# One row of the second MLP matrix in two pieces: 80 partitions on five DMA engines early, 48 as the last transfer

## The chip, the cores and the metric

The kernel runs on one core of a Trainium2 chip. The metric is the device time of one execution in microseconds, the median over runs. TensorE (PE) multiplies matrices and has a separate path that loads weights (PEld); VectorE (DVE), ScalarE (ACT) and GpSimd (POOL) do the rest of the arithmetic; SyncE (SP) issues all the DMAs of this kernel. A DMA is carried out by up to 16 DMA engines, each of which takes a share of it and works through its own queue in order.

## What is computed

The reference is a gated sum of an attention branch over a sliding window of cached keys and values (one query per sequence, 8 sequences, 32 query heads on 16 key heads, the last 2048 positions) and a small MLP:

```python
def _A_ref(x, k_cache, v_cache, wq, wo):
    W = min(4096, max(256, Sk // 4))            # 2048 of 8192
    q = (x @ wq).reshape(B, Sq, Hq, Dh).transpose(0, 2, 1, 3)
    k = jnp.repeat(k_cache[:, :, Sk - W:, :], rep, axis=1)
    v = jnp.repeat(v_cache[:, :, Sk - W:, :], rep, axis=1)
    p = _softmax(jnp.einsum("bhqd,bhkd->bhqk", q, k) * (Dh ** -0.5), axis=-1)
    o = jnp.einsum("bhqk,bhkd->bhqd", p, v)
    return o.transpose(0, 2, 1, 3).reshape(B, Sq, Hq * Dh) @ wo

def _B_ref(x, w1, b1, w2, b2):
    y = _layernorm(x, axis=-1)
    h = _gelu(jnp.einsum("bsd,df->bsf", y, w1) + b1)
    return jnp.einsum("bsf,fd->bsd", h, w2) + b2

g = _sigmoid((x * gate_w).sum(-1, keepdims=True))
return g * _A_ref(...) + (1 - g) * _B_ref(...)
```

Here D is 576 and F, the width of the hidden layer, is 4608. Everything is bfloat16 in memory.

## The kernel before, in words

The kernel streams some 154 MB through a few buffers of 4 MB each and computes on each as it lands. Queries and the hidden layer of the MLP come first (`q_fn`, `h_fn`). Then 16 items follow, each a 4 MB piece of the key cache and, later, a 4 MB piece of the value cache (`k_item`, `v_item`). At the end come the matrices that only the last step needs: `wo`, the output matrix of the attention, in two halves (`wo_chunk`, L832), and `w2`, the second matrix of the MLP (`m2_chunk`, L858).

`w2` has 4608 rows of 576 numbers. It is laid on 128 partitions with 36 such rows each; "row j" below means the j-th of these 36 on every partition, 128 pieces of 1,152 bytes. `M_CUTS` (L593) cuts the 36 into a piece of 24 rows, and then pieces of 8, 3 and 1. The list `stream` (L594) gives the order of the DMAs:

```python
M_CUTS = [[24], [8, 3, 1]]
stream += [("M", 0), ("W", 0), ("W", 1), ("M", 1)]
```

So after the last value item SP issues the 24 rows, the two halves of `wo` and then 8, 3 and 1 rows. Each issue is chained to the one before (`last_dma`), and waits on SP where its buffer is still being read. `take_slot` gives four buffers in turn; `wo`'s first half has a fifth place of its own.

Every product of the last step adds into one PSUM bank (`BK_ACC`), by `AccGroup` (L570): for each row a pair of matmuls, one for each half of 288 columns, with 8 columns of weights. `o_m2` chains these groups on PE in the order of their transfers, and each waits for its own DMA. When all have ended, DVE (L900) and ACT (L901) copy the two halves to `out_sb`, and SP stores them (L903).

The class `_Plan` (L39) orders the operations of each engine by a simple cost model when the program is built, and turns dependencies into semaphore waits. A DMA raises its semaphore by 16 when it has landed. The storage of the kernel is one array on the chip, `arena`; `req` gives a name a place in it, and `over` lays a name over the place of another. `sel` and `sel4` are small selection matrices; PE reads them in the first part of the program only (`sel_fn`, `h_fn`).

Of the kernel before, what the change touches and what calls it, by code (L numbers as in the profile page):

```python
# [6 lines left out]
BF = mybir.dt.bfloat16  # L7
F32 = mybir.dt.float32
ACTF = mybir.ActivationFunctionType
ALU = mybir.AluOpType  # L10
# [28 lines left out]
class _Plan:  # L39
# [10 lines left out]
    def add(self, eng, fn, deps=(), name=None, cost=0.1, after=(), prio=0):  # L50
        op = _Op(eng, fn, deps, name, cost, after=after, prio=prio)
        op.idx = len(self.all)
        self.all.append(op)
        return op

    def dma(self, eng, fn, semkey, nbytes, deps=(), name=None, after=(), prio=0):
        op = _Op(eng, fn, deps, name, self.DMA_ISSUE, after=after, is_dma=True, dma_sem=semkey, nbytes=nbytes, prio=prio)
        op.idx = len(self.all)
        self.all.append(op)
        return op  # L60
# [106 lines left out]
def _pst(t):  # L167
    return t.ap().ap[0][0]
# [23 lines left out]
        tile_size=(128, 128), tile_position=(0, 0)))  # L192


def build_kernel(nc, A_x, A_k_cache, A_v_cache, A_wq, A_wo, B_x, B_w1, B_b1, B_w2, B_b2, gate_w, out):
    B, Sq, D = A_x.shape
    _, Hkv, Sk, Dh = A_k_cache.shape
# [2 lines left out]
    W = min(4096, max(256, Sk // 4))  # L200
# [8 lines left out]
    ND = 4  # L209
    SE = 4 * W  # L210
    DE = 2 * SE
    FC, FT = 4, 36
# [12 lines left out]
    with ExitStack() as es:  # L225
        R = {}
        aoff = [0]

        def req(name, nelem, dt, align=64):
            sz = 2 if dt == BF else 4  # L230
            o = aoff[0] + ARENA_BASE
            o = (o + align - 1) // align * align - ARENA_BASE
            R[name] = (o, nelem, dt)
            aoff[0] = o + nelem * sz

        def over(name, base, off, nelem, dt):
            R[name] = (R[base][0] + off, nelem, dt)
            assert off + nelem * (2 if dt == BF else 4) <= R[base][1] * (2 if R[base][2] == BF else 4)
# [12 lines left out]
        req("idf8", 8, F32)  # L251
        req("dg", 16, F32)
        req("ones8", 128, F32)
        req("sel", 4 * 128, BF)
        req("sel4", 128, BF)
        req("cols", 16, F32)
        req("xT", 6 * 32, BF)
        req("yT", 6 * 32, BF)
# [17 lines left out]
        req("KT", 2 * SE // 2, BF)  # L276
        req("RAW", ND * DE + WOR * D, BF, 512)
        over("maskR", "PC", 0, 512, BF)
        over("out_sb", "PC", 1024, D, BF)
        over("KT2", "RAW", 2 * ND * DE, SE, BF)  # L280
        over("x_sb", "BD", 0, D, BF)
# [14 lines left out]
        arena = es.enter_context(nc.sbuf_tensor("arena", [128, (aoff[0] + 1) // 2], BF))  # L296
        AST = _pst(arena)
        arena_f = arena.bitcast(F32)

        def aoffs(name):  # L300
            return R[name][0] // 2
# [4 lines left out]
        def view(name, parts=128):  # L306
            o, n, dt = R[name]
            a = arena[0:parts, o // 2: o // 2 + (n * (2 if dt == BF else 4)) // 2]
            if dt == F32:
                a = a.bitcast(F32)  # L310
            return a
# [8 lines left out]
        sel = view("sel").rearrange("p (c m) -> p c m", c=4)  # L320
# [4 lines left out]
        sel4 = view("sel4", FC)  # L325
# [6 lines left out]
        hT = view("hT").rearrange("p (t b) -> p t b", b=32)  # L332
# [19 lines left out]
        def slot(s):  # L352
            return RAW[:, s * DE:min((s + 1) * DE, ND * DE + WOR * D)]
# [8 lines left out]
        def col(i, parts=128):  # L362
# [10 lines left out]
        OC = 64  # L373

        eng_sems = {e: es.enter_context(nc.semaphore("sem_" + e)) for e in ENGS}
        dma_keys = ["x", "g", "b", "b2", "wq", "w1", "out"] + ["s%d" % i for i in range(ND + 1)] + ["t%d" % i for i in range(5)]
        dma_sems = {k: es.enter_context(nc.semaphore("dma_" + k)) for k in dma_keys}

        P = _Plan()
        add, dma = P.add, P.dma  # L380
# [7 lines left out]
                   deps=[o_idf], name="r8", cost=0.2)  # L388
# [141 lines left out]
        o_selp = add("pe", sel_fn, deps=[o_qt, o_sel, o_xg], name="sel_pe", cost=0.9, prio=9)  # L530
# [20 lines left out]
        o_hp = add("pe", h_fn, deps=dw1 + db + [o_yT, o_xT, o_gcol, o_homg, o_sel4, o_obl], name="h_pe", cost=5.0)  # L551
# [10 lines left out]
        o_hT = add("dve", lambda e: e.transpose(view("hT"), bass.AP(arena, offset=aoffs("hb"), ap=[[AST, 128], [1, FT], [FT, 32]])), deps=[o_hf], name="hT", cost=1.3)  # L562
# [23 lines left out]
        NU = NG * NT  # L586
        stream, nk = [], 0
        for vi in range(NU):
# [1 line left out]
                stream.append(("K", nk))  # L590
                nk += 1
            stream.append(("V", vi))
        M_CUTS = [[24], [8, 3, 1]]  # L593
        stream += [("M", 0), ("W", 0), ("W", 1), ("M", 1)]  # L594

        last_dma = [d_w1r]
# [9 lines left out]
        def take_slot():  # L606
            n = n_slot[0]
            n_slot[0] += 1
            return (1, 2, 0, 3)[n % ND]
# [13 lines left out]
        def query(g):  # L623
            qb_done[g] = []
            for a in range(4):
                def fn(e, a=a):
                    dst = bass.AP(arena, offset=32 * a * AST + aoffs("qbd") + 640 * (g % 2) + 32 * a + 16, ap=[[AST, 32], [160, 4], [1, 16]])
                    src = bass.AP(arena, offset=32 * a * AST + aoffs("q4") + 32 * (NB_ * g + a // 2) + 16 * (a % 2), ap=[[AST, 32], [256, 4], [1, 16]])
                    return e.tensor_copy(dst, src)  # L629
                qb_done[g].append(add("pool", fn, deps=o_q4 + [o_qz, qk_unit.get(NT * (g - 1) - 1)], name="qr%d_%d" % (g, a), cost=0.3))  # L630
# [213 lines left out]
        o_m2, o_bias = [], []  # L844
# [10 lines left out]
        def bias(i):  # L855
            o_bias.append(AccGroup("m2_b", [(ob[:, 0:8], b2_sb), (ob[:, 8:16], b2_sb)], [d_b2, o_obl, o_obh], cost=0.6, after=[o_hp]).op)

        def m2_chunk(ci):  # L858
            s = take_slot()
            j = sum(sum(c) for c in M_CUTS[:ci])  # L860
            at = 0
            src = B_w2.rearrange("(p j) n -> p (j n)", j=FT)
            ops = []
            for n, jn in enumerate(M_CUTS[ci]):
                d = dma("sp", (lambda j=j, jn=jn, at=at: lambda e: e.dma_start(slot(s)[:, at * D:(at + jn) * D], src[:, j * D:(j + jn) * D]))(),
                        "t%d" % (sum(len(c) for c in M_CUTS[:ci]) + n), 128 * jn * D * 2, deps=slot_free[s] if n == 0 else [], name="d_w2_%d_%d" % (ci, n), after=last_dma[-1:])
                last_dma.append(d)
# [4 lines left out]
                j, at = j + jn, at + jn  # L872
            slot_free[s] = ops

        query(0)
        bias(0)
        for kind, i in stream:
            {"K": k_item, "V": v_item, "W": wo_chunk, "M": m2_chunk, "B": bias}[kind](i)

        seq = []  # L880
        for t in range(NU):
# [31 lines left out]
def bass_gated_mix__sliding_block_cached__mixer_channel_mlp__decode_kernel(  # L913
    nc: bass.Bass,
    A_x: bass.AP,
    A_k_cache: bass.AP,
    A_v_cache: bass.AP,
    A_wq: bass.AP,
    A_wo: bass.AP,
    B_x: bass.AP,  # L920
    B_w1: bass.AP,
    B_b1: bass.AP,
    B_w2: bass.AP,
    B_b2: bass.AP,
    gate_w: bass.AP,
    out: bass.AP,
):
    build_kernel(nc, A_x, A_k_cache, A_v_cache, A_wq, A_wo, B_x, B_w1, B_b1, B_w2, B_b2, gate_w, out)
# [28 lines left out]
```

## Time and profile before

| what | value |
|---|---|
| median of 3 runs | 364.45 us |
| the runs | 364.45, 364.46, 364.18 us |
| span of the profiled execution (first to last instruction) | 363.0 us |
| PE, busy share of the span | 82% |
| DVE | 64% |
| ACT | 46% |
| read from memory | 154.29 MB, 425 GB/s over the span |
| hardware queue of the DMAs, share of 16 engines | 98.8% |

The page gives the span of the profiled execution and no separate time for it; the medians lie 1.45 us above the span, for what is around the first and last instruction. The slices of the page are 9.1 us each, so the tail of the program, in which the last transfers land and are multiplied, is one slice or less. The timeline, the chain of waits and the windows show it closer. In the rows of the timeline the first number is the start, the second the length in microseconds, and the brackets tell how long the engine was idle and what released it. In the rows of the windows come the stretch, its length, the busy time of five engines with their instructions, the granted clock of PE, the share of DMA engines that were busy, and GB/s. In the rows of issues the last number is the time from issue to landing, which counts the queue in front.

### The profile page before, as it was taken

To read this page: it belongs to the slowest core of one execution; us is meant where nothing else is said; L and a number is where in the kernel's file an instruction comes from. 1 tells how busy PE (TensorE), PEld (TensorE's weight loads), DVE (VectorE), ACT (ScalarE), POOL (GpSimd) and SP (SyncE) were. 2 spreads that over 40 slices of the span, in tenths; PEclk is the share of its full clock that TensorE was granted. 3 is DMA by queue.
4 is the path that set the end of the run, shared out by engine and by line. 5 is a ranking of instruction groups with operands and counts; after the bars stand their busy time and mean duration, and the time that the engine had idled before them with its cause. 6 is when DMAs were issued, how large, how long until landed. Compare 5 with 4: busy or idle time off the path is not lost.

```text
span 363.0 us, 4821 instructions
## 1 busy us (share of the span) xinstructions
PE 297.9 (82%) x1954; PEld 125.3 (35%) x1423; DVE 231.4 (64%) x166; ACT 168.6 (46%) x130; POOL 22.9 (6%) x52
## 2 busy tenths in 40 slices
PE   0456366999999979998897979997989698999875
PEld 0111000434252615242433417150615152436742
DVE  0452989576666694929385768566675949295720
ACT  1022106656647463663637373838374554656000
POOL 9032030000010000000100000000000000003000
PEclk9976598999999998999999989999999999999999
DMA  8999999999999999999999999999999999999996
GB/s 347 436 437 406 455 412 455 412 455 412 450 415 451 415 451 413 441 426 441 426 441 426 435 430 437 430 437 428 437 430 437 430 435 430 437 430 433 415 430 257
DMA packets 6102, 154.45 MB, mean 426 GB/s; under 512 B 694, under 2 KB 840, under 8 KB 1228
## 3 DMA queue, kind: packets, MB, share of 16 engines
q1 hardware_dynamic: 6092, 154.30, 98.8%
q8 instruction: 8, 0.13, 0.1%
q14 instruction: 2, 0.02, 0.0%
HBM read 154.29 MB, written 0.01 MB: 425 GB/s over the span
## 4 chain that ended last, share of the span: by engine, by line
DMA 56%; DVE 27%; PE 14%; issue 1%; ACT 1%; SPq 0%; POOL 0%
DMA arena<-in_A_k_cache_dram 47%; DVE arena L718 21%; PE ps L175 6%; DMA arena<-in_B_w_dram 6%; DMA arena<-in_A_x_dram 3%; DVE arena L668 2%; PE ps L188 2%; PE ps L755 2%; PE ps L732 2%; DVE arena L645 1%; PE ps L501 0%; PE ps L579 0%; DVE arena L557 0%; DVE arena L521 0%; ACT arena L536 0%
## 5 line engine op out<-in xcount | busy, mean ns | idle before, releaser
L718 DVE STREAM_TRANSPOSE arena<-arena 128x4096 f32<-128x4096 f32 (+1 forms) x34 | 141.7, 4175 | 21.9 <-DMA arena<-in_A_k_cache_dram 21.9
L674 ACT ACTIVATE arena<-arena 32x2048 bf16<-32x2048 bf16 x60 | 114.5, 1908 | 71.4 <-DVE arena L668 42.9
L175 PE MATMUL ps<-arena 128*128 128x512 bf16 (+3 forms) x531 | 136.1, 402 | 0.0
L188 PE MATMUL ps<-arena 128*128 x840 | 109.5, 277 | 7.3 <-issue 1.2
L188 PEld LDWEIGHTS ps<-arena 128*128 x840 | 81.4, 97 | 34.3 <-issue 19.0
L732 PE MATMUL ps<-arena 128*128 128x512 bf16 x128 | 51.4, 401 | 27.6 <-DVE arena L718 26.1
L645 DVE TENSOR_REDUCE arena<-ps 128x1 f32<-128x2048 f32 x16 | 36.7, 2291 | 53.8 <-PE ps L175 53.8
L732 PEld LDWEIGHTS ps<-arena 128*128 128x128 bf16 x128 | 12.5, 98 | 131.7 <-issue 75.3
L649 ACT ACTIVATE arena<-ps,arena 128x2048 bf16<-128x2048 f32 x16 | 40.7, 2543 | 0.5
L646 ACT ACTIVATE arena<-arena 128x1 f32<-128x1 f32 x16 | 3.2, 203 | 63.5 <-DVE arena L645 63.5
L755 PE MATMUL ps<-arena 128*128 128x256 bf16 x184 | 25.3, 272 | 1.1 <-DVE arena L663 1.1
L755 PEld LDWEIGHTS ps<-arena 128*128 128x128 bf16 x184 | 16.9, 99 | 18.8 <-issue 14.6
L668 DVE STREAM_TRANSPOSE arena<-arena 128x1024 f32<-128x1024 f32 x15 | 18.1, 1205 | 2.9 <-ACT arena L649 2.9
L579 PE MATMUL ps<-arena 128*8 128x288 bf16 (+1 forms) x140 | 9.6, 286 | 4.0 <-DMA arena<-in_A_wo_dram 3.3
L739 POOL MEMSET arena<- 128x4096 f32 x1 | 3.5, 3511 | 148.2 <-PE ps L175 148.2
L685 PE MATMUL ps<-arena 128*128 128x512 bf16 x16 | 6.5, 407 | 6.5 <-ACT arena L649 5.2
L629 POOL COPY arena<-arena 32x64 bf16<-32x64 bf16 x16 | 3.7, 229 | 123.3 <-PE ps L175 122.4
L901 ACT ACTIVATE arena<-ps 8x288 bf16<-8x288 f32 x1 | 0.4, 402 | 19.5 <-PE ps L579 19.5
L422 DVE COPY arena<-arena 8x128 bf16<-8x128 bf16 x2 | 0.5, 228 | 13.9 <-DMA arena<-in_A_x_dram 13.9
L579 PEld LDWEIGHTS ps<-arena 128*8 128x8 bf16 (+1 forms) x140 | 5.8, 86 | 9.9 <-DMA arena<-in_A_wo_dram 3.3
L900 DVE CAST arena<-ps 8x288 bf16<-8x288 f32 x1 | 0.4, 446 | 12.3 <-PE ps L579 12.3
L557 DVE TENSOR_TENSOR arena<-arena 128x1152 f32<-128x1152 f32 x1 | 1.4, 1358 | 9.7 <-ACT arena L555 9.7
(106 smaller groups left out, 94.0 us busy)
## 6 DMA issues: line engine op xcount, KB each, us to landing
arena<-in_A_k_cache_dram SPq DMA_DIRECT2D x16, 4096.0 KB, 28.7
arena<-in_A_v_cache_dram SPq DMA_DIRECT2D x16, 4096.0 KB, 25.5
arena<-in_B_w_dram SPq DMA_DIRECT2D x1, 4608.0 KB, 22.0
arena<-in_A_wo_dram SPq DMA_DIRECT2D x2, 2304.0 KB, 23.8
arena<-in_A_wq_dram SPq DMA_DIRECT2D x1, 4096.0 KB, 12.6
arena<-in_B_w_dram SPq DMA_DIRECT2D x1, 3456.0 KB, 24.1
arena<-in_B_w_dram SPq DMA_DIRECT2D x1, 1152.0 KB, 22.3
arena<-in_B_w_dram SPq DMA_DIRECT2D x1, 576.0 KB, 23.0
```

The lines of the kernel that those rows point to most:

```text
L175: return e.add_instruction(mybir.InstMatmult(name=nc.get_next_instruction_name(), engine=mybir.EngineType.PE, ins=[e.lower_ap(rhs), e.lowe ...
L188: return e.add_instruction(mybir.InstMatmult(name=nc.get_next_instruction_name(), engine=mybir.EngineType.PE, ins=[rhs, lhsT], outs=[e.low ...
L579: ins = e.matmul(ps[32 * j:32 * j + 8, BK_ACC, 0:JN], lhsT, rhs[:, JN * j:JN * j + JN], start=False, stop=True, skip_group_check=True, til ...
L629: return e.tensor_copy(dst, src)
L645: mx = add("dve", lambda e: e.tensor_reduce(out=k(g, MX + x), in_=scores, axis=AXL.X, op=ALU.max), deps=[qk_unit[t]], name="mx%d" % t, cos ...
L649: ex = add("act", lambda e: e.activation(out=bass.AP(arena, offset=aoffs("P"), ap=[[AST, 128], [64, 32], [1, 2], [2, 32]]), in_=ps[:, 0:4, ...
L668: pc = add("dve", lambda e: e.transpose(view("PC").bitcast(F32), view("P").bitcast(F32)), deps=[ex] + (sp_done[t - 1][0] if t else [o_acc0 ...
L674: return e.activation(out=bass.AP(arena, offset=32 * a * AST + aoffs(home) + 64 * a, ap=[[AST, 32], [256, 32], [1, 64]]), in_=bass.AP(aren ...
L685: mm = e.matmul(*args, start=True, stop=False, skip_group_check=True) if n == 0 else held_matmul(nc, e, *args, start=True, stop=False, ski ...
L718: return e.transpose(bass.AP(arena_f, offset=foffs(base) + 2048 * h0, ap=[[AST // 2, 128], [1, 2048 * nh]]), bass.AP(arena_f, offset=foffs ...
L732: mm = e.matmul(*args, start=False, stop=True, skip_group_check=True) if rc == 0 else held_matmul(nc, e, *args, stop=True, skip=True)
L755: return e.matmul(dst, bass.AP(arena, offset=aoffs(home) + 256 * q + ee, ap=[[AST, 128], [2, 128]]), slot(s).rearrange("p (r k d) -> p r k ...
```

## The change

Row 35 of `w2`, until now the last transfer, is read in two transfers of its own into a place of its own. Partitions 0 to 79 are issued right behind the 24-row piece, in front of `wo`, with the access pattern grouped as 5 times 16 partitions. Partitions 80 to 127 are issued as the last transfer. One group of two matmuls (`m2_x`) waits for both and stands last on PE, where the last row's group stood. The place `w2x` lies over `sel` and `sel4`, which are put side by side for it; the first transfer depends on their last readers (`o_selp`, `o_hp`).

```diff
+def grouped_read(nc, e, dst, src):
+    return e.add_instruction(mybir.InstDMACopy(
+        name=nc.get_next_instruction_name(), engine=mybir.EngineType.SP, queue="qSPDynamicHW", mode="Copy",
+        ins=e.lower_ap_dma(src), outs=e.lower_ap_dma(dst), oob_is_err=True, cce_op=ALU.bypass))
...
-        req("sel", 4 * 128, BF)
-        req("sel4", 128, BF)
+        req("selb", 5 * 128, BF)
...
+        over("sel", "selb", 0, 4 * 128, BF)
+        over("sel4", "selb", 1024, 128, BF)
+        over("w2x", "selb", 0, D, BF)
...
-        M_CUTS = [[24], [8, 3, 1]]
+        M_CUTS = [[24], [8, 3]]
...
+        w2x = view("w2x")
+        X_LOW = (5, 16)
+        d_w2x = []
+
+        def row_part(i):
+            n, m = X_LOW
+            p0, p1 = ((0, n * m), (n * m, 128))[i]
+            dst = bass.AP(arena, offset=p0 * AST + aoffs("w2x"), ap=[[AST, p1 - p0], [1, 1], [1, D]])
+            src = B_w2.rearrange("(p j) n -> p (j n)", j=FT)[p0:p1, (FT - 1) * D:FT * D]
+            if i == 0:
+                src = src.rearrange("(n m) c -> n m c", n=n)
+                d = dma("sp", lambda e: grouped_read(nc, e, dst, src), "w2x", (p1 - p0) * D * 2, deps=[o_selp, o_hp], name="d_w2x%d" % i, after=last_dma[-1:])
+            else:
+                d = dma("sp", lambda e: e.dma_start(w2x[p0:p1, :], src), "w2x", (p1 - p0) * D * 2, name="d_w2x%d" % i, after=last_dma[-1:])
+            d_w2x.append(d)
+            last_dma.append(d)
+            if i == 1:
+                o_m2.append(AccGroup("m2_x", [(hT[:, FT - 1, 0:8], w2x)], [o_hT, d], cost=0.2, after=o_m2[-1:]).op)
+
+        stream = stream[:2 * NU] + [("M", 0), ("R", 0), ("W", 0), ("W", 1), ("M", 1), ("R", 1)]
```

More of the change, by code (lines that the diff above doesn't have):

```diff
@@ L375, in build_kernel @@
         eng_sems = {e: es.enter_context(nc.semaphore("sem_" + e)) for e in ENGS}
-        dma_keys = ["x", "g", "b", "b2", "wq", "w1", "out"] + ["s%d" % i for i in range(ND + 1)] + ["t%d" % i for i in range(5)]
+        dma_keys = ["x", "g", "b", "b2", "wq", "w1", "w2x", "out"] + ["s%d" % i for i in range(ND + 1)] + ["t%d" % i for i in range(5)]
         dma_sems = {k: es.enter_context(nc.semaphore("dma_" + k)) for k in dma_keys}
@@ L877, in build_kernel @@
         for kind, i in stream:
-            {"K": k_item, "V": v_item, "W": wo_chunk, "M": m2_chunk, "B": bias}[kind](i)
+            {"K": k_item, "V": v_item, "W": wo_chunk, "M": m2_chunk, "B": bias, "R": row_part}[kind](i)
         seq = []
```

## The prediction

> **What bounds the kernel now.** I read the page first (engines, DMA, queues), then the chain of waits for the last 26 us, the timeline of the tail, the issues, and the DMA share in short windows.
>
> ```profile
> span 363.0 us, 4821 instructions
> DMA  8999999999999999999999999999999999999996
> q1 hardware_dynamic: 6092, 154.30, 98.8%
> q8 instruction: 8, 0.13, 0.1%
> DMA packets 6102, 154.45 MB, mean 426 GB/s; under 512 B 694, under 2 KB 840, under 8 KB 1228
> ```
>
> The 16 DMA engines are busy in every slice but the last, so the span is 154.3 MB at one engine's pace, plus the few microseconds in which the last bytes land, are multiplied and go out. The change moves no byte in or out of that sum; it only says which engine carries the last row, and when. So it can act in the tail alone.
>
> ```profile
> 337.03 22.31 DMA arena<-in_B_w_dram
> 359.34 0.04 issue
> 359.38 1.71 PE ps L579 x24
> 361.10 0.02 issue
> 361.12 0.45 DVE arena L900
> ```
>
> The chain ends on the *eight-row* piece of w2, not on the last row. That piece lands at 359.34, and from there the chain is 24 matmuls on PE without a break, then the eviction and the store. The timeline shows the later pieces inside these 1.71 us:
>
> ```profile
> 356.65 2.13 PE L579 MATMUL ps<-arena 128*8 128x288 bf16 x32 [1.46 <-DMA arena<-in_A_wo_dram]
> 359.38 0.83 PEld L579 LDWEIGHTS ps<-arena 128*8 128x8 bf16 x16 [0.93 <-DMA arena<-in_B_w_dram]
> 359.38 1.70 PE L579 MATMUL ps<-arena 128*8 128x288 bf16 x24 [0.61 <-DMA arena<-in_B_w_dram]
> 360.42 0.22 PEld L579 LDWEIGHTS ps<-arena 128*8 128x8 bf16 x6 [0.21 <-DMA arena<-in_B_w_dram]
> 360.79 0.09 PEld L579 LDWEIGHTS ps<-arena 128*8 128x8 bf16 x2 [0.15 <-DMA arena<-in_B_w_dram]
> 361.12 0.45 DVE L900 CAST arena<-ps 8x288 bf16<-8x288 f32 x1 [12.34 <-PE ps L579]
> 361.61 0.32 SPq L903 DMA_DIRECT2D out_dram<-arena  x1
> L579 PE MATMUL ps<-arena x24: 286/286/287, 359.4 to 360.8; 128*8 128x288 bf16 x24
> ```
>
> One row of w2 is a pair of matmuls (two halves of 288 columns). The 32 matmuls at 356.65 are 16 pairs in 2.13 us; less the 0.286 of the last one, 15 steps take 1.84, so one pair follows another in 0.123 us. The three-row piece starts at 360.42. Its three pairs hold PE until 360.42 + 3 x 0.123 = 360.79, and 360.79 is when the last row's pair starts. That pair was released by its DMA, says the row, but PE could not have taken it sooner than about 0.01 us before: landing and pace meet.
>
> ```profile
> 337.03 0.80 SPq L865 DMA_DIRECT2D arena<-in_B_w_dram  x2
> 337.40 0.91 SPq L865 DMA_DIRECT2D arena<-in_B_w_dram  x2
> arena<-in_B_w_dram SPq DMA_DIRECT2D x1, 1152.0 KB, 22.3
> arena<-in_B_w_dram SPq DMA_DIRECT2D x1, 432.0 KB, 23.0
> arena<-in_B_w_dram SPq DMA_DIRECT2D x1, 144.0 KB, 22.9
> ```
>
> The three-row piece is issued at 337.40 and lands 23.0 later, at 360.40; the one-row piece lands some 0.37 later (loads at 360.42 and 360.79). It has 128 partitions, 8 rows of 1,152 bytes on each of 16 engines, so such a row costs an engine 0.37 / 8 = 0.046 us. The mean rate gives nearly the same: 9,216 bytes at 426 / 16 GB/s are 0.35 us.
>
> The engines do not finish together:
>
> ```profile
> 358.80:359.20 0.40, 0.00 (x0) 0.00 (x0) 0.00 (x0) 0.00 (x0) 0.00 (x0) 1.00 0.75 294
> 359.20:359.60 0.40, 0.22 (x4) 0.18 (x6) 0.00 (x0) 0.00 (x0) 0.00 (x0) 1.00 0.63 251
> 359.60:360.00 0.40, 0.40 (x12) 0.28 (x7) 0.00 (x0) 0.00 (x0) 0.00 (x0) 1.00 0.47 179
> 360.00:360.40 0.40, 0.40 (x10) 0.18 (x4) 0.00 (x0) 0.00 (x0) 0.00 (x0) 1.00 0.34 118
> 360.40:360.80 0.40, 0.40 (x12) 0.20 (x8) 0.00 (x0) 0.00 (x0) 0.00 (x0) 1.00 0.00 0
> ```
>
> The last but one column is the DMA share. 0.75, 0.63, 0.47 and 0.34 of 16 are 12, 10, 7.5 and 5.4 busy engines; at 360.4 all are dry. About half have nothing left 0.6 to 1.5 us before the others. The eight instruction packets of the page (0.13 MB, so 16 KB each) are a likely cause: eight, and about eight engines are late.
>
> **The change, part by part.** *Removed: the 128-partition last row.* Each engine loses 8 rows behind the three-row piece, 8 x 0.046 = 0.37 us.
>
> *Added at the end: 48 partitions*, 3 rows an engine if all 16 share it: 0.14 us. On an engine outside the five, the last landing moves from 360.74 (0.05 before the loads at 360.79) to 360.40 + 0.14 = 360.54, 0.23 earlier by 5 x 0.046. Everything ahead of it (both halves of the output matrix, the eight and the three rows) lands there as before.
>
> *Added in front of the output matrix: 80 partitions on five engines*, 16 rows each, 16 x 0.046 = 0.74 us. On these five, both halves of wo and the eight and three rows land 0.74 later than they did there, and the end comes 0.74 - 0.23 = 0.51 later. That costs nothing as long as each of the five is 0.74 ahead of the last engine. From the windows, engines dry by about 359.65 have that, some seven or eight of 16. No view numbers the engines. Strung together one after another, the packet records of the trace make 16 streams: the one with the one-partition loads of the start runs dry early, and the late ones are those that took an instruction packet. The other four of the five this leaves open in part; I take them as early, and the cost as 0, against 0.74 if one of them is the last.
>
> *SP issues one DMA more*, between the 24-row piece and wo:
>
> ```profile
> 321.52 0.33 SPq L865 DMA_DIRECT2D arena<-in_B_w_dram  x1
> 329.90 0.81 SPq L836 DMA_DIRECT2D arena<-in_A_wo_dram  x2
> SPq L836 <- PE ps L175: 8.0, 1, 8.0
> arena<-in_B_w_dram SPq DMA_DIRECT2D x1, 3456.0 KB, 24.1
> ```
>
> Its 0.33 to 0.4 us fall into the 8.0 us in which SP waits for PE ahead of wo: nothing. Without that wait, and with 24.1 us of queue ahead of any landing, it would still be covered. The new issue's own waits (the selection and the hidden-layer matmuls) are over since the start. It lands near 346, and its reader runs at 360.8. The output store stays last on SP behind one issue as before.
>
> *PE.* The number of matmuls stays; the last pair reads another buffer and waits for one semaphore to count both parts. Behind that wait stands only the eviction. The pair is ready at 360.54 + 0.05 = 360.59, but PE's three pairs hold it until 360.79, since the three-row piece lands at 360.40 as before. So the earlier landing buys 0.00 to 0.01 us. Even if every piece lay ready, 12 pairs from 359.38 would end at 359.38 + 11 x 0.123 + 0.286 = 361.02 against 361.08 now (359.38 + 1.70): 0.06 is the bound on any gain behind the eight rows.
>
> *Buffer.* The row's place overlays the two selection matrices, whose last reader is done 300 us before: 0.
>
> Writes to the SBUF side are the unknown. Before, nearly every byte comes in a 128-partition load on 16 engines; a load of 80 partitions on five isn't in it. Below: 0. Above: eight rows more for some engine's partitions, 8 x 0.046 = 0.37. I take 0, as the row for 16 engines at 426 GB/s shows no sign of a shared limit.
>
> [...]
>
> Sum: 0 + 0 + 0 - 0.00. Span 363.0 now; the runs' median is 364.45, 1.45 more lies around the span and isn't touched. Forecast 364.45.
>
> **Rivals.**
> 1. *One of the five is a late engine* (slower). The three rows then land at 360.40 + 0.74 = 361.14, the last pair starts three pairs later, all ends 0.74 later: 365.19. It decides when one of the five is less than 0.74 ahead, and reaches that price when it is the last. For it: half the engines are late, and no view names them. Against: the streams above.
> [...]
> 3. *The 80 partitions spread over all 16 engines* (the change doesn't do what it says): 5 rows an engine, all pieces up to the three rows land 0.23 later, and the end too: 364.68. Against: the grouped shape hands over five groups.
> 4. *The timed executions are bound by the last landing*, not by PE: the 0.23 counts, 364.22. Against: the chain, and pace and landing meeting at 360.79.
>
> [...]
>
> **How the numbers follow.** Forecast 0.58, rival 1 0.16, rival 2 0.08, rival 3 0.04, rival 4 0.05; 0.09 for a gain whose cause no view shows. 0.2%, 0.73 us, is about what a measurement of this kernel can tell from no change. Rivals 2 to 4 stay within it. Slower: rival 1 and 0.02 for it together with 2, 0.18. Faster 0.09, same 0.73. Range: 364.05 (rival 4 less somewhat over half of the 0.28 between the runs of before, 364.18 to 364.46) to 365.25 (rival 1 with a little over); the forecast's own is 364.2 to 364.7.
>
> **What would show it.** Right: the last landing about 0.2 earlier, the three-row loads still at 0.2 before the end of PE's run, the last pair following without a DMA as releaser, the eviction at the same distance from the eight-row landing. Rival 1: wo's halves and the eight and three rows land up to 0.74 later than SP's issue gives now. [...] Rival 3: all by 0.23, and an even stair of the DMA share. Wrong altogether: a difference ahead of 345 us, or instruction packets that fall elsewhere.

## The result, and the profile after

The changed kernel takes 365.15 us (median of 18 runs, 364.9 to 365.55) against 364.45 for the kernel before (18 runs). The ratio is 1.002, 95% interval 1.0013 to 1.0027: about 0.7 us slower, with 0.47 to 0.98 inside the interval. The span of the profiled execution went from 363.0 to 363.5.

The end of the chain of waits has the same links in the changed kernel as before, 0.53 to 0.55 us later from the landing of the eight rows on:

```profile
337.03 22.84 DMA arena<-in_B_w_dram
359.87 0.04 issue
359.91 1.73 PE ps L587 x24
...
361.67 0.45 DVE arena L929
```

SP issued the eight rows at 337.03 in both. They took 22.84 to land instead of 22.31. The timeline of the tail shows when each piece arrived; the weight loads on PE start some 0.04 us after a landing:

```profile
346.13 1.81 PEld L587 LDWEIGHTS ps<-arena 128*8 128x8 bf16 x32 [0.81 <-DMA arena<-in_B_w_dram]
...
351.62 3.41 PEld L587 LDWEIGHTS ps<-arena 128*8 128x8 bf16 x32 [2.11 <-issue]
...
357.12 1.81 PEld L587 LDWEIGHTS ps<-arena 128*8 128x8 bf16 x32 [1.74 <-DMA arena<-in_A_wo_dram]
...
359.91 0.83 PEld L587 LDWEIGHTS ps<-arena 128*8 128x8 bf16 x16 [0.99 <-DMA arena<-in_B_w_dram]
...
360.97 0.34 PEld L587 LDWEIGHTS ps<-arena 128*8 128x8 bf16 x8 [0.23 <-DMA arena<-in_B_w_dram]
```

Two rows of before that were not shown yet are the counterparts of the first two:

```profile
345.67 1.81 PEld L579 LDWEIGHTS ps<-arena 128*8 128x8 bf16 x32 [0.36 <-DMA arena<-in_B_w_dram]
...
351.19 1.84 PEld L579 LDWEIGHTS ps<-arena 128*8 128x8 bf16 x32 [2.14 <-issue]
```

In order of arrival the pieces are late by 0.46 (24 rows), 0.43 and 0.48 (the halves of the output matrix), 0.53 (eight rows) and 0.55 (three rows). Most of the loss is there with the 24 rows. These are issued *ahead* of the new load (at 321.49, the new load at 321.87), so that no engine has one of its rows in front of them in its own queue. Something slows engines that carry nothing new.

The windows say more, and so do the packet records of the traces, which keep start, length and size of every packet. The new load has five landings, at 344.94 to 346.28 us, where the 24 rows have 16; its 80 packets run from 343.57 to 345.44. So the stretch from 344 to 346 us is the one in which the five engines carry most of their 80 partitions, while others still finish the 24 rows or have begun the output matrix. The last two numbers are the busy share of the DMA engines and GB/s; the first row is before, the second the changed kernel:

```profile
344.00:346.00 2.00, 1.92 (x21) 1.44 (x21) 0.37 (x1) 0.00 (x0) 0.00 (x0) 1.00 1.05 452
```

```profile
344.00:346.00 2.00, 1.60 (x15) 1.18 (x13) 0.36 (x1) 0.00 (x0) 0.00 (x0) 1.00 1.03 355
```

The engines are as busy as before, and move less. How much less these rows tell only roughly: they count each packet whole in the window in which it begins, so that a share can pass 1, and what straddles the edges of a short window weighs. With the packets cut at the edges, the records of the two traces give 0.86 MB before and 0.71 MB after from 344 to 346 us, and from 343 to 347 us 1.73 MB against 1.56. These 0.17 MB take 0.39 us at the 432 GB/s that before has in this stretch, most of the delay of the 24 rows. The new load is only 92 KB, and they are counted in the 1.56: beside its own bytes, each of them cost nearly two bytes of others.

The lengths of the packets show who is slowed. From 343 to 347 us of before, every packet of the 24 rows takes 1,025 ns and every packet of the output matrix 686. In the changed kernel 16 packets are under way at 345.0 us, one on each engine: seven of the 24 rows, 1,186 to 1,362 ns long, eight of the output matrix, 782 to 960 ns, and one of the new rows, 74 ns instead of the 51 that a packet of the last row takes in before. So all 16 engines are slowed. The seven that still carry the 24 rows have no new row: their packets end at 345.28 to 345.44, and by 345.28 all but two of the 80 new packets have begun. They are the last of the 16 to land their share: at 345.92 to 346.09 us, against 345.36 to 345.63 before. From 347 to 350 us the packets of the output matrix take 686 to 689 ns again.

The last row's pair is no longer released by a DMA: the row of the timeline at 360.97 holds the weight loads of the last four rows, two for each, without a break.

SP issued the grouped load in 0.87 us, ahead of a wait of 7.1 us:

```profile
321.87 0.87 SPq L196 DMA_DIRECT2D arena<-in_B_w_dram  x1
SPq L844 <- PE ps L175: 7.1, 1, 7.1
```

### The profile page after: what moved, and what is told of

Its sections match the earlier page's. It is cut to its first block, busy times and chain, and to the rows that moved or that the text cites. A ratio compares the mean times of both kernels' runs of the same rounds, so it can differ in the third digit from the quotient of the medians.

```text
span 363.5 us, 4803 instructions
## 1 busy us (share of the span) xinstructions
PE 296.9 (82%) x1935; PEld 125.5 (35%) x1423; DVE 231.5 (64%) x166; ACT 168.7 (46%) x130; POOL 23.0 (6%) x52
## 4 chain that ended last, share of the span: by engine, by line
DMA 54%; DVE 22%; PE 21%; issue 1%; SPq 1%
DMA arena<-in_A_k_cache_dram 48%; DVE arena L726 18%; PE ps L175 9%; DMA arena<-in_B_w_dram 6%; PE ps L188 6%; PE ps L740 3%; PE ps L763 2%; DVE arena L676 2%; DVE arena L653 1%; DVE arena L802 1%; PE ps L587 0%; PE ps L693 0%; DVE arena L929 0%; SPq L425 0%; SPq L420 0%
## 5 line engine op out<-in xcount | busy, mean ns | idle before, releaser
L740 PE MATMUL ps<-arena 128*128 128x512 bf16 x122 | 48.9, 401 | 18.7 <-DVE arena L726 17.2
L587 PE MATMUL ps<-arena 128*8 128x288 bf16 (+1 forms) x140 | 11.2, 316 | 3.0 <-DMA arena<-in_A_wo_dram 1.8
L693 PE MATMUL ps<-arena 128*128 128x512 bf16 x11 | 4.4, 399 | 5.2 <-ACT arena L657 5.2
L802 DVE SCALAR_TENSOR_TENSOR arena<-ps,arena 128x256 f32<-128x256 f32 x12 | 5.7, 476 | 2.8 <-PE ps L763 2.7
```

The costliest lines, as they stand in the source:

```text
L587: ins = e.matmul(ps[32 * j:32 * j + 8, BK_ACC, 0:JN], lhsT, rhs[:, JN * j:JN * j + JN], start=False, stop=True, skip_group_check=True, til ...
L693: mm = e.matmul(*args, start=True, stop=False, skip_group_check=True) if n == 0 else held_matmul(nc, e, *args, start=True, stop=False, ski ...
L740: mm = e.matmul(*args, start=False, stop=True, skip_group_check=True) if rc == 0 else held_matmul(nc, e, *args, stop=True, skip=True)
L802: fn = lambda e, src=src, w=w: e.scalar_tensor_tensor(out=X2, in0=src, scalar=w, in1=X2, op0=ALU.mult, op1=ALU.add)
```

## Experiments

Two theories are set against each other. Theory A: the five engines write many partitions that other engines write in a 128-partition load (128 packets with 16 landings are 8 an engine, 40 for five, so 40 of the 80 at the least if all take the same share), and the writes of all engines slow down meanwhile. Theory B: one of the five is itself a late engine (the first rival of the prediction). Each experiment was timed against the kernel before on its own chip.

### The load alone, in two ways

The kernel before, unchanged in its transfers, with bytes loaded that nobody reads. First the 80 partitions as in the change, in one load (`e1`); then the same number of pieces on five engines, to 40 partitions (0 to 19 and 32 to 51), twice, in four loads of four pieces an engine (`e2`). No record shows which partitions an engine writes in a 128-partition load, so whether these 40 are the five's there was not shown. The edit, cut:

```diff
+        def extra_read(i, p0, n, m, place):
+            src = B_w2.rearrange("(p j) n -> p (j n)", j=FT)[p0:p0 + n * m, (FT - 1) * D:FT * D].rearrange("(n m) c -> n m c", n=n)
+            dst = bass.AP(arena, offset=p0 * AST + aoffs(place), ap=[[AST, n * m], [1, 1], [1, D]])
...
+        X_PARTS = [(0, 5, 16, 'selb')]                     # e1
+        X_PARTS = [(0, 5, 4, 'selb'), (32, 5, 4, 'selb'), (0, 5, 4, 'q4'), (32, 5, 4, 'q4')]   # e2
+        stream = stream[:2 * NU] + [("M", 0), ("X", 0), ("W", 0), ("W", 1), ("M", 1)]
```

> The kernel before, with all its transfers as they were, and one load more that nobody reads: the same 80 partitions of row 35 on five engines, at the same place between the 24 rows and the output matrix. Theory A (five engines that write many other partitions take time from the writes of all engines): the 24 rows already land about 0.46 us later, and all pieces behind them too, as in the changed kernel; the end comes 0.5 us later, time 0.4 to 0.8 us over before. Theory B (one of the five is itself the last engine and simply carries 16 rows more): the 24 rows land as before, since they are ahead of the load in every queue; from the output matrix on all lands up to 0.74 us later.

> As the experiment with the extra 80 partitions, with the same bytes on the same five engines (16 pieces of 1,152 bytes each), but to other partitions: 0 to 19 and 32 to 51, four to each engine and twice over, in four loads. Theory A: if these are the partitions that the five engines write in a 128-partition load anyway, nobody else's writes are met; all landings within 0.1 us of before, time within 0.15 us of before. Theory B, and any theory in which the bytes or the reads of five busy engines are the cost whatever their destination: the same as with the 80 partitions, 0.4 to 0.8 us over before. [...]

Measured: the 80 partitions cost 0.46 us (365.02 against 364.56; ratio 1.0015, 1.0006 to 1.0024). The same bytes to 40 partitions cost nothing that can be told (364.65; 1.0003, 0.9994 to 1.0011). The window from 344 to 346 us, first with the 80 partitions, then with the 40 twice:

```profile
344.00:346.00 2.00, 1.49 (x14) 1.08 (x12) 0.48 (x1) 0.00 (x0) 0.00 (x0) 1.00 0.98 335
```

```profile
344.00:346.00 2.00, 1.94 (x21) 1.44 (x20) 0.37 (x1) 0.00 (x0) 0.00 (x0) 1.00 1.13 475
```

and the arrival of the 24 rows, in the same order:

```profile
346.11 1.81 PEld L586 LDWEIGHTS ps<-arena 128*8 128x8 bf16 x32 [0.90 <-DMA arena<-in_B_w_dram]
```

```profile
345.65 1.81 PEld L586 LDWEIGHTS ps<-arena 128*8 128x8 bf16 x32 [0.34 <-DMA arena<-in_B_w_dram]
```

0.44 late and 0.02 early. Both rates are rough for the reason given above; with the packets cut at the edges, 0.71 MB move from 344 to 346 us with the 80 partitions and 0.85 MB with the 40 twice, against 0.86 before. At 345.0 us all 16 packets under way are longer than in before with the 80 partitions, and none is with the 40. Theory B falls: it has the 24 rows on time, as they are issued ahead of the load, and with the 80 partitions they are 0.44 late. With the 40 twice five engines carry 16 pieces more as well (20 landings for the four loads, where the one load has five), and nothing behind them is late either: the eight rows start at 359.39 against 359.38. That they are the same five was not shown, as no record numbers the engines.

### What is read, or what is written

The second experiment read other rows of memory than the first. This one writes as the second and reads as the first; if what is written is the cost, all should land as in `e2` (the source, cut, otherwise as there):

```diff
-            src = ...[p0:p0 + n * m, (FT - 1) * D:FT * D].rearrange("(n m) c -> n m c", n=n)
+            src = ...[0:80, (FT - 1) * D:FT * D].rearrange("(n q m) c -> n q m c", n=n, q=4)[:, i]
```

> [...] If it is what they read (rows of memory that five engines walk through): as with the extra 80 partitions, the 24 rows 0.45 us late and time 0.4 to 0.6 us over before.

Measured: 364.63 against 364.53 us, ratio 1.0004, 0.9995 to 1.0014; the weight loads of the 24 rows start at 345.68, and every packet of the output matrix from 343 to 347 us takes 686 ns. So what is read does not matter here.

That it is the destination is shown with one thing left open. The 80 partitions come as one load with 16 pieces an engine, the 40 twice, in both runs, as four loads with four; no run wrote partitions 0 to 19 and 32 to 51 in one load, or 0 to 79 in fours. Two measurements speak for the destination even so: the last row of before, one load with eight pieces on every engine, takes 51 ns a piece, and one load with eight pieces on five engines, to partitions 0 to 39, leaves 392 GB/s where before has 433 (`e9`, below).

### The early load left out

The line that matters; the run also zeroes the part of the place that is then not loaded, and makes the late load wait for the last readers of the place:

```diff
-        stream = stream[:2 * NU] + [("M", 0), ("R", 0), ("W", 0), ("W", 1), ("M", 1), ("R", 1)]
+        stream = stream[:2 * NU] + [("M", 0), ("W", 0), ("W", 1), ("M", 1), ("R", 1)]
```

> The changed kernel without its early load: 80 partitions of row 35 are left out and only the 48 come, as the last transfer (the product of that row is then not the reference's). Theory A: no slow stretch, all pieces land as before; the last piece lands 0.2 us earlier, but the matmul pairs of the three rows hold PE, so the end moves by less than 0.06 us; time within 0.15 us of before. If the last landing sets the end after all: 0.2 us under before. If the 48 partitions at the end are themselves the cost: 0.4 us or more over before.

Measured: 364.57 against 364.56 us, ratio 1.0002, 0.9993 to 1.0011. The 48 partitions at the end are not the cost. The tail:

```profile
359.39 0.83 PEld L588 LDWEIGHTS ps<-arena 128*8 128x8 bf16 x16 [1.05 <-DMA arena<-in_B_w_dram]
...
360.44 0.34 PEld L588 LDWEIGHTS ps<-arena 128*8 128x8 bf16 x8 [0.22 <-DMA arena<-in_B_w_dram]
361.14 0.45 DVE L930 CAST arena<-ps 8x288 bf16<-8x288 f32 x1 [12.42 <-PE ps L588]
```

The last pair follows without a wait, so the last piece was there before PE came to it, and yet the eviction starts at 361.14 against 361.12. The lighter last transfer alone, with nothing paid for it, buys nothing. In this profile the second half of the output matrix comes 0.11 early (356.53 against 356.64) and the eight rows 0.01 late: the late load may delay the landings around it by a tenth of a microsecond too, which one profile does not make certain.

### The 80 partitions on all 16 engines

```diff
-                src = src.rearrange("(n m) c -> n m c", n=n)
-                d = dma("sp", lambda e: grouped_read(nc, e, dst, src), "w2x", ...
+                d = dma("sp", lambda e: e.dma_start(w2x[p0:p1, :], src), "w2x", ...
```

> The changed kernel with the 80 partitions not grouped, so that all 16 engines take five of them each. [...] Theory B: the 24 rows land as before, the rest 0.23 us later, time 0.23 us over before.

Measured: 365.69 against 364.56 us, ratio 1.0039, 1.0023 to 1.0055, 1.13 us over before, where theory B has 0.23. The 24 rows are 0.42 late (346.09), and the first half of the output matrix 1.23 (352.42 against 351.19): the engines stay slow long after the 80 partitions are in. The stretch from 346 to 350 us, before and with 16 engines:

```profile
346.00:350.00 4.00, 3.37 (x62) 2.16 (x50) 1.71 (x6) 0.00 (x0) 0.00 (x0) 1.00 1.01 433
```

```profile
346.00:350.00 4.00, 3.70 (x64) 2.44 (x56) 1.82 (x6) 0.00 (x0) 0.00 (x0) 1.00 0.98 378
```

The kernel with the extra 80 partitions has 433 GB/s here as before has. With 16 engines the packets of the first half of the output matrix settle at 766 to 768 ns instead of 686, on all engines, and those of the second half are back at 686.

### Low or high partitions on four engines

Two edits of the changed kernel; the second has the first line too:

```diff
-        X_LOW = (5, 16)
+        X_LOW = (4, 16)                                         # e5: 0 to 63 early
-            p0, p1 = ((0, n * m), (n * m, 128))[i]
+            p0, p1 = ((128 - n * m, 128), (0, 128 - n * m))[i]   # e6: 64 to 127 early
```

> The changed kernel with four groups of 16: partitions 0 to 63 early on four engines, 64 to 127 last. If only the engines whose partitions are written are held up: the engines that write 64 to 127 go on as before, so that some of the late ones land in time and some late; the last landing of the 24 rows 0.2 to 0.4 us late, the three rows 0.2 to 0.4. If the whole fabric is held up: all 0.4 us late as with five engines.

> The changed kernel with four groups of 16 at the other end: partitions 64 to 127 early on the same four engines, 0 to 63 last. [...] If the destination doesn't matter: as with partitions 0 to 63.

Measured: 365.32 and 365.27 against 364.53 us (1.0022, 1.0013 to 1.0032; 1.002, 1.001 to 1.0029). In the profile of the high partitions the 24 rows are 0.68 late (346.35). In that of the low ones they are 0.80 late (346.47), but there the whole tail runs late from before: SP issues the eight rows at 337.38 instead of 337.03, so 0.45 remain. High partitions delay the 24 rows more (0.68 against 0.45), but the times don't differ. Whether only the engines are held up whose partitions are written, the packet records tell: with partitions 0 to 63 alone, all 16 packets under way at 345.5 us are longer than before's, 11 of the output matrix (739 to 962 ns), four of the 24 rows (1,122 to 1,289) and one new row (69). With 64 to 127 alone it is the same at 345.0 us. So no engine is spared, whichever half is written.

### One engine, and half the load

The kernel with the extra load, with other partitions:

```diff
-        X_PARTS = [(0, 5, 16, 'selb')]
+        X_PARTS = [(64, 17, 1, 'selb')]    # e8: 17 partitions on one engine
+        X_PARTS = [(0, 5, 8, 'selb')]      # e9: 40 partitions on five
```

> The kernel before with one extra load of 17 partitions (64 to 80), which one engine carries alone, 0.8 us of its time. If writes to partitions that belong to other engines hold up those engines for as long as they last: the 24 rows land 0 to 0.2 us late, time 0 to 0.25 us over before, a fifth to a third of what five engines cost. If it needs several engines at once: nothing, time within 0.1 us.

> The kernel before with half the extra load: partitions 0 to 39 of row 35 on the same five engines, 8 rows each. If the held-up writes cost in proportion to the rows that go to other engines' partitions: half of what 80 partitions cost, the 24 rows 0.2 to 0.3 us late, time 0.15 to 0.35 us over before. If starting such a load is the cost: as with 80 partitions, 0.4 us or more.

> The load of 17 partitions on one engine once more: its runs lay between 364.5 and 367.4 us, while the profile showed 0.15 us. If the spread belongs to the kernel (one engine with 17 rows more may or may not be the last), it is there again; if it was a disturbed stretch, the runs lie within 0.6 us of each other and 0 to 0.3 us over before.

Measured: one engine 366.42 against 364.53 us (1.0048, 1.0024 to 1.0071; runs from 364.48 to 367.44), and again 366.16 against 364.59 (1.0052, 1.0037 to 1.0066; 365.22 to 367.23). Half the load on five engines 366.05 against 364.59 (1.0038, 1.0022 to 1.0054; 364.6 to 367.22). Less is moved than in the extra 80 partitions and more is lost, in a wide scatter: the loss isn't in proportion. The first profile of the one-engine load, of an execution of 364.69 us, has the first half of the output matrix at 351.39, 0.20 late; the second, of 365.22 us, has it at 352.18, 0.99 late, with 387 GB/s from 346 to 350 us where before has 433. So the same kernel falls into the slow stretch or doesn't. The profile of half the load shows it too, as with 16 engines:

```profile
346.00:350.00 4.00, 3.53 (x64) 2.30 (x52) 1.66 (x6) 0.00 (x0) 0.00 (x0) 1.00 0.99 392
```

### The early part cut to partitions 0 to 19 and 32 to 51

The change itself, with 40 partitions early (0 to 19 and 32 to 51, as in the second extra load) and 88 last:

```diff
+            for p in (((0, 5, 4, True), (32, 5, 4, True)), ((20, 3, 4, False), (52, 3, 4, False), (64, 16, 4, False)))[i]:
+                row_piece(*p)
```

> [...] If the writes to other engines' partitions were the whole loss: the 24 rows, both halves of the output matrix and the eight rows land within 0.1 us of before. [...] Time 0 to 0.35 us over before, so less than half of the changed kernel's loss. If the loss had another cause in the new transfers (their number, their shape, the shared semaphore): 0.6 us or more.

Measured: 364.97 against 364.56 us, ratio 1.0011, 1.0002 to 1.002. All that comes early is on time; the tail isn't:

```profile
345.59 1.81 PEld L587 LDWEIGHTS ps<-arena 128*8 128x8 bf16 x32 [0.33 <-DMA arena<-in_B_w_dram]
...
360.58 0.22 PEld L587 LDWEIGHTS ps<-arena 128*8 128x8 bf16 x6 [0.28 <-DMA arena<-in_B_w_dram]
361.10 0.09 PEld L587 LDWEIGHTS ps<-arena 128*8 128x8 bf16 x2 [0.30 <-DMA arena<-in_B_w_dram]
```

The 24 rows start 0.08 earlier than before and the output matrix too (351.11 and 356.56); the three rows are 0.16 late and the last row 0.31. The loss of the early part is gone, and the end has a smaller one. The 88 partitions there come in three loads instead of one, and the packets of the last row take 51 ns as in before; what makes the end late was not separated. No version tried beats the kernel before.

## Why the prediction was wrong

**The step that failed** is the one on the writes: "I take 0, as the row for 16 engines at 426 GB/s shows no sign of a shared limit." That row shows only 128-partition loads on 16 engines; it could not show what a load of 80 partitions on five does. In place of the 0, the five engines' 80 partitions slowed all 16 engines and made the 24 rows 0.46 us late; the extra load alone, with nothing else changed, made them 0.44 late and the kernel 0.46 us slower. As many pieces on five engines to partitions 0 to 19 and 32 to 51 moved the 24 rows by -0.02 and 0.01, whichever rows they read.

**The bound for it was too low as well.** It was 0.37, eight rows of 0.046 on one engine, as if a row from another engine took just its own time from the engine it holds up. Measured were 0.46 at the 24 rows and 0.55 at the three rows. The packet records show 0.17 MB less moved around a load of 92 KB, and every engine slowed, not only one.

Why partitions 0 to 19 and 32 to 51 went free (0.85 MB in the two microseconds, against 0.86 before) and 0 to 79 took this to 0.71 was not shown. Nor do the runs tell how all 16 engines come to be slowed where 64 partitions are written.

**The rival that had the right time had the wrong cause.** A late engine among the five was priced at 365.19, beside the measured 365.15. But the 24 rows were late ahead of any new row, and five engines with 16 pieces more delayed nothing when the pieces went to partitions 0 to 19 and 32 to 51 (the eight rows at 359.39, against 359.38). That the measured time lies inside the stated range, which was stretched for this rival, is luck. The chances of 0.08 and 0.02 for rival 2 were for a delay of up to 0.37, the author's estimate: no run shows that term, and in its place the runs showed the 24 rows 0.46 late and a loss of 0.70 us.

**What held.** The last landing was not what ended the kernel: without the early load the last piece was there before PE came to it, and the eviction moved by 0.02. PE's pairs after the three rows are the pace, as worked out. SP's extra issue took 0.87 us rather than 0.33 to 0.4, and still lay within SP's wait for PE. The 80 partitions went to five engines and not to all 16: the trace of the extra load has five landings for it, where a 128-partition load has 16, and with all 16 the kernel is slower still (365.69). The instruction packets, 0.88 to 0.97 us each, fit the late engines: seven had come when the 24 rows of before landed, and seven of the 16 engines landed them late (345.36 to 345.63, the others by 344.84); the eighth came at 349.9, and eight landed the eight rows late (359.00 to 359.34, the others by 358.54).

**What stays open.** How a load of five engines to partitions 0 to 79 slows all 16. Why the 16-engine load, the one-engine load and half the load leave the engines slow after they have ended (378 to 392 GB/s from 346 to 350 us, with most packets at 766 to 791 ns until the first half of the output matrix is in), the one-engine load in one of its two profiles and not in the other, and why their times scatter by up to 3 us; the destination alone does not explain that the smaller loads cost more. And not all of the 0.70 us is accounted for: the extra load alone costs 0.46, the profiled tail shows 0.55, and the rest lies within the intervals.

## What to carry to other kernels

Where the DMA engines are the bound, as here (98.8% of 16 engines), ask what else slows when work is moved to engines that finish early: in this kernel 80 partitions in one load on five engines made the 24 rows 0.44 late, and as many pieces to partitions 0 to 19 and 32 to 51 in four loads did not (0.02 early). Look at GB/s beside the busy share, and at the length of packets of one size: here the share was equal (1.05 and 1.03) while packets grew from 686 to as much as 974 ns. A piece that is late though it stands *ahead* of the new load in its queue, as the 24 rows here by 0.46, points to something shared with other engines: packets were longer on all 16. And before a last transfer is made lighter, check whether the consumer's pace has not already met its landing; the prediction worked out 0.01 us to win here, and the run without the early load won nothing.

## What the runs showed of the hardware

A load of 92 KB on five DMA engines, to partitions 0 to 79 with 16 in a row from each engine, made the packets of all 16 engines longer (686 ns to as much as 974, and 1,025 to as much as 1,362) and took the bytes moved in 2 us from 0.86 to 0.71 MB. The same amount on as many engines to partitions 0 to 19 and 32 to 51, four in a row from each engine and in four loads, did not (0.85 MB, all packets of the output matrix at 686 ns). Smaller loads of partitions in a row (17 on one engine, 40 on five) cost more in time than 80 on five, with a wide scatter: 1.6 to 1.9 and 1.5 us against 0.46.
